# Convolution in 32-token blocks with two lag steps per matmul, in a kernel that runs attention and a long convolution side by side

## The chip, the cores and the metric

One core of a Trainium2 chip. The metric is the device time of one execution in microseconds; quoted times are medians. Ratios are computed as the mean time of one kernel's fast runs over the mean of the other's in the same rounds, so they are not quite the ratio of the medians beside them. One kernel's executions can differ by a per cent, so differences under 1% are not read as effects. A run counts as slow when its time is over 1.5% above the fastest run of the same kernel; the others are fast. The medians are over all runs of a kernel, slow ones included.

## The reference, cut to what matters

```python
x = A_x                                       # 1 x 2048 x 448
g = sigmoid((x * gate_w).sum(-1, keepdims=True))
a = attention(x, wq, wk, wv, wo)              # 16 heads of 28, one key/value head
K = einsum("dn,dnl,dn->dl", C, exp(dt*A*l), dt*B).real   # 448 channels x 2048 taps, 256 modes
y = causal_convolution(u, K) + u * Dskip      # every channel has its own taps
return g * a + (1 - g) * y
```

The device kernel reads A_x for both inputs. It computes the convolution as matmuls, channel by channel: shifted copies of the taps (`T`) are the moving operand, the tokens (`U`) the stationary one, also called the weights. The moving operand of one matmul is called a stream below. PSUM is the memory that takes the results of matmuls (`psS`, `psX` and `psB` in the profiles).

## The kernel before: the parts that matter

Every operation is handed to a small static scheduler, together with an expected duration in ns. The scheduler fixes the order of instructions on each engine before the kernel runs. A wrong duration gives no wrong result, but a poor order.

```python
def conv(self, c):                      # 16 channels, bank 5 of PSUM
    for k in range(4):
        gi = 4 * c + k; s = gi % self.NTR
        self.tload(gi)                  # 128 x 8 KB into one of four T buffers
        for m in range(1, 16, 2):
            def mm(e, ...):
                for j in range(4):      # four channels, one per 32-column tile
                    r = e.matmul(ps.v(32 * j, 33 - m, po + 128 * k, [[1, 128]]),
                                 self.U.v(0, P, (m - 1) * D + 4 * gi + j, [[D, 33 - m]]),            # weights
                                 self.T.v(0, P, s * 4096 + (960 - 64 * m) * 4 + j, [[4, 128]]),      # moving: step 4 elements = 8 bytes
                                 start=(m == 1), stop=(m == 15), tile_position=(0, 32 * j), ...)
            pg.op("pe", mm, 112, ...)   # scheduled as 112 ns per four matmuls
    # VectorE multiplies by (1 - g) into cst, ytr flips and sums on TensorE, VectorE adds to O
```

TensorE also runs the scores (L967 in the profile of before), probability times value (L985), the making of the taps (L792) and the projections (L676, L877). ScalarE runs the exponentials (L977). VectorE builds the tables from which the taps are made (L759, L762, L767, L776, L778). All of it is interleaved in one schedule.

## Time and profile before

| | before |
|---|---|
| time | 539.37 us (537.78 to 539.81) |
| busy: TensorE / VectorE / ScalarE | 484.8 / 483.9 / 487.5 us of a span of 537.2 |
| mean granted TensorE clock | 0.921 |
| convolution matmuls on TensorE | 142 us |
| scores + probability-value on TensorE | 144 + 78 us |
| TensorE idle | 39 us |

The granted clock is the share of TensorE's full clock that the chip let it run at; in all 14 clock records of this trace it is either full or half (1.00 or 0.50). The last three rows are read from the trace. Each matmul is given the time to the start of the next one, at most its own record, and what remains between the first matmul and the last is idle. This counts overlapped matmuls once, which the group rows of the page do not do. Three engines at 90% each is the main thing to see: by these shares none of the three stands out as the bound. The chain that ended last is shared by them too:

```profile
PE 47%; ACT 36%; DVE 12%; DMA 2%; issue 1%; POOL 1%; DVEq 0%; POOLq 0%
```

### The profile page before, as it was taken

What the parts mean: (1) busy time and instruction counts of PE and PEld (TensorE: products, weight loads), DVE (VectorE), ACT (ScalarE), POOL (GpSimd) and SP (SyncE); (2) the same over time, 40 slices, a digit from 0 to 9 for tenths busy, and PEclk for the clock granted to TensorE, in tenths of its full rate; (3) what the DMA queues carried; (4) which work ended last, traced back from release to release, by engine and by line L of the source; (5) the groups of instructions that cost most, each with busy time, mean ns of one, the idle gap of its engine ahead of it and who ended that gap; (6) DMA issues with size and microseconds to landing.
All of it is one profiled execution on the core that took longest, in us unless ns stands there. A gap on an engine that the chain in (4) does not pass through costs nothing.

```text
span 537.2 us, 18418 instructions
## 1 busy us (share of the span) xinstructions
PE 484.8 (90%) x8229; PEld 243.8 (45%) x8229; DVE 483.9 (90%) x1168; ACT 487.5 (91%) x428; POOL 4.9 (1%) x17
## 2 busy tenths in 40 slices
PE   6778888999999899999999999999999998998893
PEld 5411132553545444554545445554455543544452
DVE  4978899998999999999999999999999999999023
ACT  4599998998999999999999999999999999999960
POOL 3000000000000000000000000000000000000000
PEclk9855566997999999999999999999999999889997
DMA  8735445777798867779898896778877796697954
GB/s 232 145 79 137 138 139 207 245 285 299 249 327 297 303 230 237 253 265 345 304 337 320 262 332 238 242 260 319 309 296 267 285 393 220 176 388 254 350 188 137
DMA packets 42266, 138.16 MB, mean 257 GB/s; under 512 B 8168, under 2 KB 24476, under 8 KB 27852
## 3 DMA queue, kind: packets, MB, share of 16 engines
q1 hardware_dynamic: 40396, 135.71, 73.7%
q10 hardware_dynamic: 1792, 1.29, 0.8%
q8 instruction: 64, 1.05, 0.8%
q14 instruction: 14, 0.11, 0.1%
HBM read 133.01 MB, written 3.85 MB: 255 GB/s over the span
## 4 chain that ended last, share of the span: by engine, by line
PE 47%; ACT 36%; DVE 12%; DMA 2%; issue 1%; POOL 1%; DVEq 0%; POOLq 0%
ACT expT L977 35%; PE psS L967 13%; PE psS L853 12%; PE psB L985 8%; PE psX L792 6%; PE psX L676 2%; DMA T<-KP_scratch 2%; DVE tab L767 2%; DVE tmp L762 2%; DVE tab L759 2%; PE psS L504 1%; PE psX L877 1%; PE psX L831 1%; DVE O L883 1%; DVE tab L776 1%
## 5 line engine op out<-in xcount | busy, mean ns | idle before, releaser
L977 ACT ACTIVATE expT<-psS 128x1536 bf16<-128x1536 f32 (+1 forms) x410 | 470.8, 1254 | 19.0 <-PE psB L985 12.9
L967 PE MATMUL psS<-qT,kT 29*128 29x512 bf16 x1024 | 170.6, 412 | 29.6 <-ACT expT L977 27.2
L853 PE MATMUL psS<-T,U 128*26 128x128 bf16 (+7 forms) x3584 | 157.9, 303 | 0.6 <-DMA T<-KP_scratch 0.5
L853 PEld LDWEIGHTS psS<-T,U 128*26 128x26 bf16 (+7 forms) x3584 | 113.9, 152 | 35.3 <-issue 28.2
L985 PE MATMUL psB<-expT,vaug 128*32 128x512 bf16 x1024 | 108.8, 417 | 1.4 <-ACT gtok L643 1.3
L967 PEld LDWEIGHTS psS<-qT,kT 29*128 29x128 bf16 x1024 | 39.6, 92 | 124.4 <-ACT expT L977 92.8
L762 DVE TENSOR_TENSOR tmp<-tab,mbf 128x2048 bf16<-128x2048 bf16 (+4 forms) x140 | 78.0, 563 | 0.0
L759 DVE TENSOR_TENSOR tab<-tab,mbf 128x2048 bf16<-128x2048 bf16 (+4 forms) x140 | 77.9, 563 | 0.0
L767 DVE TENSOR_TENSOR tab<-tab,tmp 128x2048 bf16<-128x2048 bf16 (+4 forms) x140 | 77.8, 563 | 0.0
L792 PE MATMUL psX<-tab 128*32 128x96 bf16 x1792 | 54.8, 268 | 1.3 <-issue 1.2
L985 PEld LDWEIGHTS psB<-expT,vaug 128*32 128x32 bf16 x1024 | 26.6, 95 | 64.2 <-issue 60.8
L792 PEld LDWEIGHTS psX<-tab 128*32 128x32 bf16 x1792 | 41.2, 116 | 14.2 <-issue 9.0
L776 DVE TENSOR_TENSOR tab<-tab,mbf 128x2048 bf16<-128x2048 bf16 x28 | 34.0, 1216 | 0.0
L778 DVE TENSOR_TENSOR tab<-tab,mbf 128x2048 bf16<-128x2048 bf16 x28 | 34.0, 1213 | 0.0
L861 DVE TENSOR_TENSOR cst<-psS,omq 128x512 bf16<-128x512 f32 x28 | 19.0, 680 | 15.7 <-PE psS L853 15.5
L717 DVE TENSOR_TENSOR msq<-mst 128x256 f32<-128x256 f32 x63 | 26.2, 416 | 0.0
L676 PE MATMUL psX<-xT,Wq 112*128 112x512 bf16 x64 | 21.7, 436 | 0.4 <-DVE O L838 0.2
L727 DVE CAST mbf<-mst 128x256 bf16<-128x256 f32 x70 | 20.1, 288 | 0.1
L720 DVE TENSOR_TENSOR mst<-msq 128x128 f32<-128x128 f32 x70 | 19.7, 282 | 0.0
L723 DVE SCALAR_TENSOR_TENSOR mst<-mst 128x128 f32<-128x128 f32 x63 | 17.8, 283 | 0.0
L804 DVE TENSOR_REDUCE kstg<-psX 128x128 bf16<-128x256 f32 x28 | 11.7, 418 | 4.2 <-PE psX L792 4.1
L730 DVE TENSOR_SCALAR mbf<-mst 128x128 bf16<-128x128 f32 x70 | 15.3, 218 | 0.0
(112 smaller groups left out, 255.8 us busy)
## 6 DMA issues: line engine op xcount, KB each, us to landing
T<-KP_scratch SPq DMA_DIRECT2D x112, 1024.0 KB, 7.8
rdenB<-R_scratch SPq DMA_DIRECT2D x60, 64.0 KB, 3.8
U<-in_A_x_dram SPq DMA_DIRECT2D x3, 896.0 KB, 5.4
tab<-in_A_x_dram SPq DMA_DIRECT2D x4, 448.0 KB, 6.9
O<-Z_scratch SPq DMA_DIRECT2D x1, 1792.0 KB, 13.6
KP_scratch<-kstg SPq DMA_DIRECT2D x28, 64.0 KB
xT<-in_A_x_dram SPq DMA_DIRECT2D x1, 1792.0 KB, 9.2
U<-Z_scratch SPq DMA_DIRECT2D x1, 896.0 KB, 8.0
```

Of the source, the lines that this page charges most:

```text
L676: pg.op("pe", lambda e, T=T: e.matmul(px, self.Wq.v(0, DT, T * 512 + g * 128, [[1, 128]]), self.xT.v(0, DT, T * S + 512 * qc, [[1, 512]]), ...
L717: pg.op("dve", lambda e, k=k: e.tensor_tensor(msq.v(0, P, 0, [[1, 2 * BW]]) if k > 1 else msq.v(0, P, 0, [[BW, 2], [1, BW]]), src_both(k - ...
L759: pg.op("dve", lambda e, d=dst, a=src, ra=ra, w=w: e.tensor_tensor(d, a, mbf.v(0, P, ra, [[8, 16], [0, 2 * w], [1, 4]]), ALU.mult), el(n, ...
L762: pg.op("dve", lambda e, a=src, rb=rb, w=w: e.tensor_tensor(tmp.v(0, P, so, [[4 * w, 32], [1, 4 * w]]), a, mbf.v(0, P, rb, [[4, 32], [0, w ...
L767: pg.op("dve", lambda e, d=dst, t=t2: e.tensor_tensor(d, d, t, ALU.add), el(n, 1.92), rd=[("tmp", s), ("tab", s, lv + 1)], wr=[("tab", s, ...
L776: pg.op("dve", lambda e: e.tensor_tensor(ua, src, mbf.v(0, P, ra, [[8, 8], [0, 64], [1, 4]]), ALU.mult), el(2048, 1.92), rd=rk + mk, wr=[( ...
L778: pg.op("dve", lambda e: e.tensor_tensor(ub, src, mbf.v(0, P, rb, [[4, 16], [0, 32], [1, 4]]), ALU.mult), el(2048, 1.92), rd=rk + mk, wr=[ ...
L792: r = e.matmul(self.psX.v(32 * g, 32, 96 * jj, [[1, 96]]), tab.v(0, P, o + 768, [[4, 32]]), tab.v(0, P, o, [[256, 3], [4, 32]]), start=(co ...
L853: r = e.matmul(ps.v(32 * j, 33 - m, po + 128 * k, [[1, 128]]), self.U.v(0, P, (m - 1) * D + 4 * gi + j, [[D, 33 - m]]), self.T.v(0, P, s * ...
L967: r = e.matmul(self.psS.v(0, P, 1536 * s + 512 * k, [[1, 512]]), kT.v(32 * h, DH + 1, 128 * kt, [[1, 128]]), qT.v(32 * h, DH + 1, 512 * qs ...
L977: pg.op("act", lambda e: e.activation(expT.v(0, P, 512 * (i0 % 10), [[1, n]]), self.psS.v(0, P, 1536 * s, [[1, n]]), AF.Exp, scale=SQ), 75 ...
L985: r = e.matmul(self.psB.v(32 * h, 32, 0, [[1, 512]]), vaug.v(0, P, 32 * kt, [[1, 32]]), expT.v(0, P, 512 * ((4 * st + h) % 10), [[1, 512]] ...
```

## The change

The intent was to take time from TensorE and to move fewer bytes: pairs of 64-column matmuls in place of groups of four of 128 (the same number of matmuls over half the columns each), T loads half as large, weights that lie contiguously, results flipped and summed by one matmul with a flip matrix, fewer blocks of table powers. The diff, cut to its core:

```diff
-KPW = 2112
+KR = 68
+KPW = 256 * KR
...
-        sizes = [4] * 7
+        sizes = [2, 5, 7, 7, 7]
...
-        pg.dma([(self.T.v(0, P, s * 4096, [[1, 4096]]),
-                 dram(self.KP, 4 * gi * KPW, [[4, 64], [4096, 2], [1, 4096]]))],
-               (128, 8192), f"T{s}", rd=[("KP", c), "pad"], wr=[("T", s)], pr=1, ns=3300)
+        pg.dma([(self.T.v(0, P, s * self.TW, [[1, self.TW]]), dram(self.KP, gi * KPW, [[KR, 128], [1, self.TW]]))],
+               (128, 4096), f"T{s}", rd=[("KP", c)], wr=[("T", s)], pr=1, ns=1700)
...
-            for m in range(1, 16, 2):
-                def mm(e, k=k, m=m, s=s, gi=gi):
-                    for j in range(4):
-                        r = e.matmul(ps.v(32 * j, 33 - m, po + 128 * k, [[1, 128]]),
-                                     self.U.v(0, P, (m - 1) * D + 4 * gi + j, [[D, 33 - m]]),
-                                     self.T.v(0, P, s * 4096 + (960 - 64 * m) * 4 + j, [[4, 128]]),
-                                     start=(m == 1), stop=(m == 15), tile_position=(0, 32 * j), skip_group_check=True)
-                pg.op("pe", mm, 112, rd=[("T", s), "U"], ...
+            for k1 in range(2):
+                pr = 2 * q + k1
+                for mg in range(2):
+                    def mm(e, mg=mg, k1=k1, pr=pr, s=s):
+                        for m in range(4 * mg, 4 * mg + 4):
+                            M = max(34, 64 - 8 * m)
+                            for par in range(2):
+                                r = e.matmul(ps.v(64 * par, M, po + 64 * pr, [[1, 64]]),
+                                             self.U.v(0, P, uo + (32 * par + e0 + pr) * UC + 8 * m, [[1, M]]),
+                                             self.T.v(0, P, s * self.TW + 8 * m + 2 * k1 + par, [[4, 2], [KR, 32]]),
+                                             start=(m == 0), stop=(m == 7), tile_position=(0, 64 * par), skip_group_check=True)
+                    pg.op("pe", mm, 118, rd=[("T", s)] + ...
...
-    def ytr(self, c):                  # 16 small matmuls with an identity, per chunk
+    def jpass(self, c):                # two matmuls with a flip matrix
```

Cut away: the staging of the input in memory and its reversed reload as `U`, the output projection as two pairs of 224 columns, the skip connection, and some constants of the scheduler. The moving operand of the change is `[[4, 2], [KR, 32]]`: its inner dimension steps 68 elements, 136 bytes. Its tiling has two column tiles (64 wide) where before had four (32 wide). And 118 ns are scheduled for four pairs, about 30 ns a pair.

## The prediction

A "line" is an aligned stretch of 16 bytes in a partition of the moving operand. A "drain" is the time that a change of tiling adds, some 100 ns in the trace of before (315 ns from start to start against 216). What TensorE does in it is not shown.

> **What bounds the kernel now.** I read the page first (busy shares, slices, chain), then the groups, the waits of ScalarE and VectorE, the timeline of one warm stretch, and the start times of single instructions. The page gives three engines at nine tenths:
>
> ```profile
> PE 484.8 (90%) x8229; PEld 243.8 (45%) x8229; DVE 483.9 (90%) x1168; ACT 487.5 (91%) x428; POOL 4.9 (1%) x17
> ...
> PEclk9855566997999999999999999999999999889997
> ```
>
> The second row is the granted TensorE clock per slice; it is about half from slice 3 to slice 7, that is roughly from 22 to 94 us. The groups say which work this is:
>
> ```profile
> L977 ACT ACTIVATE expT<-psS 128x1536 bf16<-128x1536 f32 (+1 forms) x410 | 470.8, 1254 | 19.0 <-PE psB L985 12.9
> ...
> L853 PE MATMUL psS<-T,U 128*26 128x128 bf16 (+7 forms) x3584 | 157.9, 303 | 0.6 <-DMA T<-KP_scratch 0.5
> ...
> L792 PE MATMUL psX<-tab 128*32 128x96 bf16 x1792 | 54.8, 268 | 1.3 <-issue 1.2
> ```
>
> The exponentials (L977) fill ScalarE, and it idles only 19 us in front of them. But busy time hides something: back to back, a 1536-wide exponential starts 1330 ns after the last and a 1024-wide one 901 ns (10th percentile of the starts), while their records are longer because they overlap. Summed over the loop (33.6 to 519.5 us) the starts lie 32 us above that pitch: 12 us before 136 us, where the TensorE clock is half for long, 19 us from 136 to 470, and 1.3 us in the last 50 us. So ScalarE could save at most 32 us. Who holds it up:
>
> ```profile
> ACT expT L977 <- PE psB L985: 12.9, 27, 1.4
> ACT expT L977 <- PE psS L967: 4.4, 10, 0.7
> ```
>
> Both are TensorE being late. The timeline of TensorE shows why: pieces of the convolution (L853, 28 matmuls, about 0.9 us) lie between score matmuls (L967) and probability-value matmuls (L985).
>
> ```profile
> 228.62 0.39 PE L967 MATMUL psS<-qT,kT 29*128 29x512 bf16 x2
> 228.94 0.40 PE L985 MATMUL psB<-expT,vaug 128*32 128x512 bf16 x4
> 229.16 1.03 PE L853 MATMUL psS<-T,U 128*20 128x128 bf16 x28
> 230.12 0.39 PE L967 MATMUL psS<-qT,kT 29*128 29x512 bf16 x3
> ```
>
> VectorE is as full (162.1 of 164 us between 136 and 300 us), but its share of the work ends near 492 us; then it waits for the last two convolutions:
>
> ```profile
> DVE cst L861 <- PE psS L853: 15.5, 4, 12.2
> ```
>
> After the last exponential (519.5) there are 17.7 us of tail: normalisation, projection, the last convolution (its matmuls run to 527.9) and 7.4 us of stores issued at 529.8.
>
> [...] from a row-tiled L967 to a column-tiled L985 the starts are 315 ns apart, from L985 to L853 (same tiling) 216 ns, so a change costs some 100 ns. [...] L831 (64-column tiles, 64 wide) runs a pair every 33 ns, 16 ns each. [...] The trace hints that strides matter: four concurrent L853 matmuls of 128 columns (step 8 bytes) take 124 ns from start to start, four L792 of 96 columns (step 8 bytes) 91 ns, four L985 of 512 contiguous columns 216 ns. That is 0.95 ns a column against 0.42, nearly whatever the weight columns (121 ns at 18, 126 at 30), and the same at half clock (120 to 126 and 90 ns). So the array is not the limit there. [...] In the trace 512-byte packets took 33 ns on average, 64-byte ones 11 ns: 16 against 6 bytes per ns.
>
> **The change part by part.**
> Convolution on TensorE: before, 896 groups of four by 124 ns = 111 us. After, again 28 x 128 = 3584 matmuls, but in 1792 pairs of 64 columns. If a pair runs at L831's 33 ns: 59 us, 52 less. The tiling becomes that of two columns[...]: of 246 visits, some 140 have L985 or L792 beside them; 140 x 0.1 = 14 us more. Net about -38 us of TensorE, 8% of its time.
> Weights: U becomes contiguous in time; the loads with step 896 bytes (149 ns median) should drop towards the 110 ns of L831's contiguous 64 columns. They are hidden behind the matmuls anyway.
> Flip and sum: 28 x 8 pairs x 33 ns = 7.4 us become 28 x two matmuls of 256 columns, about 6 us. Output projection: 448 columns as two pairs of 224, the same streaming; its eviction is two instructions in place of one, VectorE about +1 us in all. The skip connection gets fewer multiplies on long rows and more short adds: even.
> Master tables: 5 blocks in place of 7, hence 2 x 52 fewer VectorE instructions. L717 (256 elements, 416 ns) against L720 (128, 282 ns) gives some 150 ns fixed, about half of it overlapping the next instruction: 104 x 70 ns = -7 us. The first block is of 2 chunks, so the first tables come some 4 us sooner.
> DMA: a T load goes from 1024 KB to 544 KB, 112 times: 115 MB become 61 MB. It adds 28 loads of U with 2048 rows of 61 to 64 elements, about 126 bytes. At 15 ns a packet these are 57,000 packets / 16 x 15 ns = 54 us of queue time over the run, against some 170 us saved by T (from 325 us of 8 KB packets). No transfer should hold TensorE.
> Start: a staged transpose to memory and reversed copies; perhaps +1.5 us on the way to the first exponential.
> On the path: less TensorE work shortens the delays of the exponentials. Of the 32 us I take back 14, not all: the half-clock stretch stays, and VectorE still has 477 us of work. The tail loses about 3 us, since the last convolution ends before the last exponential and three of the four stores can go early. 539.4 - 14 - 3 + 1 = 523.
>
> **The rivals.**
> A, as above: the pair runs at 33 ns. For it: L831 does so with 64-column tiles, and the change's own scheduler costs put 118 ns on four pairs. Time 515 to 531.
> B, the strided stream sets the pace. The new moving operand steps 136 bytes, one element per 16-byte line, where the old one had two. If the limit is lines, 256 lines in 124 ns before, a pair's 128 lines take 60 ns: 1792 x 60 = 108 us, nothing gained, plus 14 us of drains, and a fixed instruction order planned for half of it. Better constants in the planner, the shorter VectorE work and the earlier tail offset this: 531 to 552, about 540. For it: the 0.95 ns does not move with the clock, and loads of weights also get slower with their step. Against: the new tiling has half the streams, and the costs written into the change.
> C, each stream has its own limit of lines: 120 ns a pair, 215 us of convolution, TensorE becomes the only bound: above 600.
> D, VectorE takes over: with ScalarE freed, its 98% in the loop stops the gain. The chunk work ended at 492 us and loses 7, so this bites only below about 515.
>
> **Range and chances.** I give A 0.5, B 0.42, C 0.08. A is faster by over 2% (below 528.6) with 0.85; B with 0.12, and slower with 0.2; C is slower. Faster 0.425 + 0.05 = 0.48, slower 0.08 + 0.08 = 0.16, within 2% 0.36. The middle of the mixture is a little above A's: 527. Range 514 to 549; C lies outside it.
>
> **What would show it.** The deciding number is the start-to-start time of two consecutive pairs of the convolution in a warm stretch: 30 to 35 ns for A, 55 to 65 for B, about 120 for C. For A the idle before exponentials falls below 12 us, the excess of their starts over the back-to-back pitch from 32 to about 18, and the last matmul of the convolution comes before the last exponential. For B these stay near 19 and 32, and PE busy stays at 480 us or more. T loads of 544 KB should land in some 5 us (7.8 before). VectorE busy should be about 477. I am wrong if the U loads make TensorE wait, if the start to the first steady exponential (33.7 us) moves by over 3 us, or if the new drains cost more than 100 ns each.

## The result, and the profile after

The changed kernel takes **693.04 us** (689.59 to 697.21, four runs) against 538.58 (535.97 to 539.81) in the same rounds: ratio 1.288, 95% interval 1.278 to 1.298. The result is correct. The prediction said 527.

The page of the changed kernel: the busy row and the granted clock, then the groups of the exponentials, the convolution, the scores, and the VectorE instruction that takes the convolution's results.

```profile
PE 624.0 (91%) x8034; PEld 343.0 (50%) x8048; DVE 489.4 (71%) x1085; ACT 496.3 (72%) x428; POOL 7.8 (1%) x15
...
PEclk9755559999877999999788997899799999855555
...
PE 68%; DVE 15%; ACT 15%; DMA 1%; issue 1%; SPq 0%
...
L1023 ACT ACTIVATE expT<-psS 128x1536 bf16<-128x1536 f32 (+1 forms) x410 | 479.6, 1240 | 158.7 <-PE psS L1013 94.3
L891 PE MATMUL psS<-T,U 128*34 128x64 bf16 (+4 forms) x3584 | 248.8, 303 | 1.0 <-issue 0.8
L1013 PE MATMUL psS<-qT,kT 29*128 29x512 bf16 x1024 | 186.6, 454 | 38.6 <-ACT expT L1023 35.4
...
L900 DVE TENSOR_TENSOR cst<-psS,omq 128x512 bf16<-128x512 f32 x28 | 19.4, 692 | 111.6 <-PE psS L891 111.6
```

TensorE alone is near nine tenths now; the exponentials wait 159 us, nearly all of it for TensorE (19 before), VectorE 112 us for the convolution alone. The convolution row grew from 157.9 to 248.8 us though every matmul has half the columns, and the mean record is 303 ns in both. The timeline of a warm stretch shows the pace (start, duration, engine, line, count):

```profile
228.78 0.40 PE L1031 MATMUL psB<-expT,vaug 128*32 128x512 bf16 x4
229.11 1.15 PE L891 MATMUL psS<-T,U 128*64 128x64 bf16 x16
...
230.19 0.39 PE L1013 MATMUL psS<-qT,kT 29*128 29x512 bf16 x2
```

Sixteen matmuls are eight pairs, and the next matmul starts 1.08 us after the first pair: with some 0.1 us of that a change of tiling, a pair every 120 ns or so. Taken pair by pair from the starts in the trace, the median is 122 ns, with 121 to 124 at every weight width from 34 to 64, and the same at full and at half clock. (Matmuls of the same pair start together.) This is the number the prediction called deciding: 30 to 35 for A, 55 to 65 for B, about 120 for C.

Where the 150 us between the two profiled spans are, by the counting of the table above (all matmuls that it does not name fit in the third row):

| TensorE, us | before | after | |
|---|---|---|---|
| convolution | 142.4 | 237.5 | +95 |
| scores + probability-value | 222.1 | 261.1 | +39 |
| all other matmuls (taps, projections, flip) | | | about +5 |
| idle | 39.2 | 49.1 | +10 |
| before the first matmul and after the last | 13.2 | 14.6 | +1 |

Most of the +39 is the clock. From start to start, a 512-column matmul of the query projection takes 216 ns at the full clock and 427 at the half, and the mean clock fell from 0.921 to 0.828: 646 of the 2048 score and value matmuls ran at half clock, against 254 before. With the times per matmul of the kernel before at each clock, that alone gives +29. The other 10 are the change of tiling: from the last value matmuls to the first of the convolution 329 ns pass in place of 227 at the full clock (546 in place of 400 at the half), 86 times. So two things are to be explained: the 122 ns, and the clock.

### The profile page after: what moved, and what is told of

Read it like the earlier page. It is cut to its first block, busy times and chain, and to the rows that moved or that the text cites. A ratio compares the mean times of both kernels' runs of the same rounds, so it can differ in the third digit from the quotient of the medians.

```text
span 687.7 us, 18049 instructions
## 1 busy us (share of the span) xinstructions
PE 624.0 (91%) x8034; PEld 343.0 (50%) x8048; DVE 489.4 (71%) x1085; ACT 496.3 (72%) x428; POOL 7.8 (1%) x15
## 4 chain that ended last, share of the span: by engine, by line
PE 68%; DVE 15%; ACT 15%; DMA 1%; issue 1%; SPq 0%
PE psS L891 34%; PE psS L1013 15%; ACT expT L1023 14%; PE psB L1031 9%; PE psX L828 4%; PE psX L709 2%; DVE tab L803 2%; DVE tab L795 1%; DVE tmp L798 1%; PE psX L918 1%; DMA tab<-in_A_x_dram 1%; DVE msq L752 1%; PE psS L531 1%; PE psX L865 1%; DVE cst L900 1%; PE psS L918 1%
## 5 line engine op out<-in xcount | busy, mean ns | idle before, releaser
L891 PE MATMUL psS<-T,U 128*34 128x64 bf16 (+4 forms) x3584 | 248.8, 303 | 1.0 <-issue 0.8
L1013 PE MATMUL psS<-qT,kT 29*128 29x512 bf16 x1024 | 186.6, 454 | 38.6 <-ACT expT L1023 35.4
L891 PEld LDWEIGHTS psS<-T,U 128*34 128x34 bf16 (+4 forms) x3584 | 197.8, 122 | 45.5 <-issue 43.2
L803 DVE TENSOR_TENSOR tab<-tab,tmp 128x128 bf16<-128x128 bf16 (+4 forms) x140 | 79.2, 566 | 0.7
L798 DVE TENSOR_TENSOR tmp<-tab,mbf 128x128 bf16<-128x128 bf16 (+4 forms) x140 | 78.9, 564 | 0.0
L795 DVE TENSOR_TENSOR tab<-tab,mbf 128x128 bf16<-128x128 bf16 (+4 forms) x140 | 78.3, 565 | 0.5
L752 DVE TENSOR_TENSOR msq<-mst 128x448 f32<-128x448 f32 (+2 forms) x45 | 23.6, 524 | 0.0
L870 DVE TENSOR_TENSOR O<-O,psX 128x256 bf16<-128x256 bf16 x28 | 11.6, 416 | 9.2 <-PE psX L865 9.1
L763 DVE CAST mbf<-mst 128x448 bf16<-128x448 f32 (+2 forms) x50 | 17.1, 342 | 0.1
L756 DVE TENSOR_TENSOR mst<-msq 128x224 f32<-128x224 f32 (+2 forms) x50 | 16.9, 338 | 0.0
```

Source lines behind the costliest of these rows:

```text
L752: pg.op("dve", lambda e, k=k: e.tensor_tensor(msq.v(0, P, 0, [[1, 2 * BW]]) if k > 1 else msq.v(0, P, 0, [[BW, 2], [1, BW]]), src_both(k - ...
L795: pg.op("dve", lambda e, d=dst, a=src, ra=ra, w=w: e.tensor_tensor(d, a, mbf.v(0, P, ra, [[8, 16], [0, 2 * w], [1, 4]]), ALU.mult), el(n, ...
L798: pg.op("dve", lambda e, a=src, rb=rb, w=w, so=so: e.tensor_tensor(tmp.v(0, P, so, [[4 * w, 32], [1, 4 * w]]), a, mbf.v(0, P, rb, [[4, 32] ...
L803: pg.op("dve", lambda e, d=dst, t=t2: e.tensor_tensor(d, d, t, ALU.add), el(n, 1.92), rd=[("tmp", lv % 2), ("tab", s, lv + 1)], wr=[("tab" ...
L891: r = e.matmul(ps.v(64 * par, M, po + 64 * pr, [[1, 64]]), self.U.v(0, P, uo + (32 * par + e0 + pr) * UC + 8 * m, [[1, M]]), self.T.v(0, P ...
L1013: r = e.matmul(self.psS.v(0, P, 1536 * s + 512 * k, [[1, 512]]), kT.v(32 * h, DH + 1, 128 * kt, [[1, 128]]), qT.v(32 * h, DH + 1, 512 * qs ...
```

## The experiments

Theory: a moving operand costs a fixed time for every new 16-byte line, in every stream by itself (the prediction's rival C). Rivals: the limit is shared by all streams (B), the smaller tiles or the weights set the pace, or the two-dimensional address. And for the rest of the loss: the half clock, the fixed order, or another engine.

### The read step: a_contig, a_steps, b_wide, b_step2

**a_contig** changes only how the moving operand of the changed kernel is read (wrong result):

```diff
-self.T.v(0, P, s * self.TW + 8 * m + 2 * k1 + par, [[4, 2], [KR, 32]])
+self.T.v(0, P, s * self.TW + 8 * m + 2 * k1 + par, [[1, 64]])
```

> The changed kernel, but the moving operand of the convolution is read contiguously (64 neighbouring elements in place of step 136 bytes); the result is wrong on purpose, everything else stays. Theory S (step): each stream of a moving operand gets one 16-byte line per 1.9 ns, so the strided pair takes 64 x 1.9 = 120 ns; contiguous, a pair takes 30 to 35 ns and the time falls from 693 to 518 to 535 us. Rival T (tiling): two column tiles of 64 with weights of 34 to 64 columns cost 120 ns a pair whatever is read; the pair stays at 120 and the time at 690. Rival R (rest): the pair goes to 33 ns, but the drains, the loads of U or the planned order hold the time above 600 us.

Measured: 568.09 us (564.05 to 574.72), before 539.22 in the same rounds, ratio 1.058 (1.048 to 1.068). A pair comes every 29 to 30 ns at the full clock (52 after the pair with the widest weights, 64 columns) and every 53 to 55 at the half; the convolution takes 87 us of TensorE in place of 237. So the step explains about 125 of the 154 us. Tiles, weights and the places of the results are the same as in the change, so they do not set the 122 ns; VectorE's instructions come in the same order too. (One of the four runs was slow.) But the time did not fall to 518-535; some 29 us above before are left for the second question.

**a_steps** gives each of the eight channel pairs of a T buffer another step (wrong on purpose, one look), each on its own source line; L892 has the change's own operand, but runs the four matmuls of one tile and then the four of the other, in place of alternating.

```diff
+if pr == 0:   r = e.matmul(*a, tv([[1, 64]]), **kw)     # L901: 2 bytes
+elif pr == 1: ... tv([[2, 64]])                         # L903: 4 bytes
+elif pr == 2: ... tv([[4, 64]])                         # L905: 8 bytes
+elif pr == 3: ... tv([[8, 64]])                         # L907: 16 bytes
+elif pr == 4: ... tv([[32, 64]])                        # L909: 64 bytes
+elif pr == 5: ... tv([[KR, 32], [4, 2]])                # L911: lag pair inside
+elif pr == 6: ... tv([[4, 2], [KR, 32]])                # L913: as in the change
+else: tile after tile                                   # L892: as in the change
```

> The changed kernel with another way of reading in each of the eight channel pairs of a chunk, each from its own source line (wrong result on purpose): step 2, 4, 8, 16 and 64 bytes; the right elements with the two lags innermost; the right elements as in the change; and as in the change but four matmuls of one tile before the four of the other. Theory S with a limit per stream: start to start of a pair 33, 33, 60, 120, 120 ns; lags innermost 80 to 100 (half of its element pairs lie in two lines); as is 120; tile after tile about 700 ns for eight matmuls in place of 480. If the limit were shared by the two streams, tile after tile would stay at 480 and step 8 bytes would take 30. Rival T: all 120. Time 590 to 640 us under S.

The groups of TensorE by line (busy us, mean ns of one record):

```profile
L892 PE MATMUL psS<-T,U 128*64 128x64 bf16 (+1 forms) x448 | 34.1, 301 | 0.0
L913 PE MATMUL psS<-T,U 128*64 128x64 bf16 (+1 forms) x448 | 34.0, 303 | 0.3 <-issue 0.3
L909 PE MATMUL psS<-T,U 128*64 128x64 bf16 (+1 forms) x448 | 32.1, 287 | 0.0
L907 PE MATMUL psS<-T,U 128*64 128x64 bf16 (+1 forms) x448 | 32.0, 294 | 0.5 <-DVE tab L803 0.5
L911 PE MATMUL psS<-T,U 128*64 128x64 bf16 (+1 forms) x448 | 26.6, 269 | 0.0
L905 PE MATMUL psS<-T,U 128*64 128x64 bf16 (+1 forms) x448 | 19.9, 237 | 0.5 <-DVE tab L795 0.3 <-DVE acc L998 0.3
L901 PE MATMUL psS<-T,U 128*64 128x64 bf16 (+1 forms) x448 | 15.5, 213 | 0.0
L903 PE MATMUL psS<-T,U 128*64 128x64 bf16 (+1 forms) x448 | 15.2, 209 | 0.0
```

The same 448 matmuls stand on every line, so the rows compare directly: equal at 2 and 4 bytes, more at 8, and from 16 bytes on a plateau. Start to start, a pair takes 29 ns at 2 bytes and 33 at 4 at the full clock (53 at the half), and at both clocks 59 at 8 bytes, 115 at 16, 110 at 64, 123 as in the change, and 90 with the lag pair inside. It stops growing at 16 bytes, the step where every column has a line of its own (115 ns, and 110 at 64 bytes). The two-dimensional address is not the point: 16 bytes in one dimension cost nearly the same. Tile after tile was a miss: eight matmuls take about 480 ns as in the alternating order, not the 700 I had written. Nor was it the test that it was meant to be. In the trace the two matmuls that start together have weights of the same width (64 and 64, then 56 and 56), and in the first half of a channel pair's matmuls each width occurs once per tile. So the two tiles ran side by side, though the kernel's text has the four of one tile first; where the order changed is not shown. By what I had written, the 480 spoke for a limit shared by the streams and the 59 ns at 8 bytes against it.

**b_wide** puts the same question to the kernel before, with four streams: a step of 64 bytes in place of 8 (wrong on purpose, one look). **b_step2** goes the other way and is correct: the taps of two channels are interleaved in memory in place of four, so the step is 4 bytes.

```diff
 # b_wide
-self.T.v(0, P, s * 4096 + (960 - 64 * m) * 4 + j, [[4, 128]])
+self.T.v(0, P, s * 4096 + j, [[32, 128]])
 # b_step2 (the stores of the taps and the T load follow the same layout, as two DMAs each in place of one)
-self.T.v(0, P, s * 4096 + (960 - 64 * m) * 4 + j, [[4, 128]])
+self.T.v(0, P, s * 4096 + j // 2 * 2048 + (960 - 64 * m) * 2 + j % 2, [[2, 128]])
```

> The kernel before, with one thing of the change put in alone: its moving operand steps 64 bytes in place of 8 (wrong result on purpose), the tiling, order, loads and weights stay. Theory S per stream: a group of four goes from 124 to 128 x 1.9 = 243 ns, the convolution from 111 to 218 us, the time from 539 to 630 to 690 us, and the granted clock falls as in the changed kernel. If lines are shared by the four streams, a group takes twice that, 490 ns, and the time passes 800. Rival T and R: no change, 124 ns and 539 us.

> The kernel before, with the taps of two channels interleaved in place of four, so that the moving operand steps 4 bytes in place of 8; right result. Theory S: four elements a line, a group of four takes max(0.42, 1.9 / 4) x 128 = 61 ns in place of 124, the convolution 55 us in place of 111, no drain added; fewer late score matmuls, time 512 to 528 us, and it beats both kernels. Under T nothing changes: 124 ns, 539 us. If VectorE is the bound behind TensorE, the group falls to 61 ns but the time stays above 530.

The convolution group and the granted clock, b_wide first:

```profile
PEclk9755669989999999999999999999999999999998
...
L853 PE MATMUL psS<-T,U 128*32 128x128 bf16 (+7 forms) x3584 | 258.8, 416 | 1.5 <-issue 1.3
```

and b_step2:

```profile
PEclk9765566995999699999898999999887997888597
...
L853 PE MATMUL psS<-T,U 128*32 128x128 bf16 (+7 forms) x3584 | 121.7, 251 | 2.5 <-DVE cst L861 0.5
```

b_wide: a group of four every 236 ns (124 before), 621.32 us, just under the 630 to 690 expected. b_step2: in the median 62 ns at the full clock with the narrowest weights, 87 with the widest, and 107 at the half clock (whether the loads of the weights, with step 896 bytes, play a part in this at the full clock, no run tests); 545.19 us, ratio 1.011 (1.005 to 1.017). That is the miss that matters: a read of the taps that took 30 us off the convolution did not make the kernel faster. (It also changed the order of instructions; see below.) And the clock went the other way than I had written: it rose in b_wide (0.941) and fell in b_step2 (0.858).

### The law inside the change, with a right result: a_pair72

If two columns share a line, the changed kernel's pair should take half the time. The lag pair goes inside, and a row has 72 lags, so that rows begin on 16 bytes; the VectorE instruction that takes the results puts the columns back in order.

```diff
-KR = 68
+KR = 72
-self.T.v(0, P, s * self.TW + 8 * m + 2 * k1 + par, [[4, 2], [KR, 32]])
+self.T.v(0, P, s * self.TW + 8 * m + 2 * k1 + par, [[KR, 32], [4, 2]])
-e.tensor_tensor(cst [[64, 8], [1, 64]], ps [[64, 8], [1, 64]], omq [[0, 8], [1, 64]], ALU.mult)
+e.tensor_tensor(cst [[64, 8], [32, 2], [1, 32]], ps [[64, 8], [1, 2], [2, 32]], omq [[0, 8], [32, 2], [1, 32]], ALU.mult)
```

> The changed kernel with the same right result, but the pair of lag steps is the inner dimension of the moving operand and a row holds 72 lags, so that consecutive columns lie 8 bytes apart (two to a 16-byte line) in place of 136. Theory 'a column costs 1.9 ns per stream when it lies in its own 16-byte line, half as much when two share one': a pair of matmuls every 58 to 64 ns at the full clock, 124 in the change; convolution 115 to 135 us in place of 237; time 585 to 615 us, less than the arithmetic 693 - 110 would give only if the half clock does not come with it. Rival 'what counts is that the address steps in two dimensions, or the jump between the rows': the lags-innermost order of 68 read 90 ns already, so it stays near 90 to 124 and the time at 640 or more.

Measured: 578.48 us (575.95 to 580.59), correct, ratio to before 1.070 (1.061 to 1.078). A pair every 60 ns, in the median, at both clocks and all weight widths. Convolution 126 us. So 115 us of the loss come back with little but another order of reading, somewhat more than expected (585 to 615 us). L911 of a_steps read in this order too, but with rows of 68 lags: every second row then begins in the middle of a 16-byte line, its pairs lie in two lines, and a pair of matmuls took 90 ns. The step inside a pair is 8 bytes in both; what differs between 90 and 60 ns is how many lines are touched, 48 or 32. The group:

```profile
L891 PE MATMUL psS<-T,U 128*34 128x64 bf16 (+4 forms) x3584 | 136.4, 237 | 3.1 <-issue 2.0
```

### One stream in the full array: b_full

a_steps left open whether the limit belongs to a stream or to all streams together. b_full reads the query projection of the kernel before (512 columns, whole array, one stream) in other steps, each input block on its own line (wrong).

```diff
+if T == 1: return e.matmul(px, w, xv([[4, 512]]), **kw)              # L681: 8 bytes
+if T == 2: return e.matmul(px, w, xv([[0, 4], [16, 128]]), **kw)     # L683: 32 bytes
+if T == 3: return e.matmul(px, w, xv([[0, 2], [2, 256]]), **kw)      # L685: 4 bytes
+return e.matmul(px, w, xv([[1, 512]]), **kw)                         # L686: contiguous
```

> The kernel before with the query projection's 512-column moving operand (full tiling, one stream) read in other steps, wrong result on purpose; each of the four input blocks has its own source line: contiguous, 4 bytes with every column pair twice, 8 bytes, and 32 bytes. If a stream is limited to one new 16-byte line per 1.9 ns whatever the tiling: about 480 ns at 8 bytes and 970 at 32. If the limit is for TensorE's whole front end (0.47 ns a line as with four streams): 216 to 240 ns at both. If two matmuls can be read at a time (0.95 ns a line): 240 and 480.

The durations, min/median/max:

```profile
L681 PE MATMUL psX<-xT,Wq x16: 610/612/636, 17.1 to 442.0; 112*128 112x512 bf16 x16
...
L683 PE MATMUL psX<-xT,Wq x16: 1075/1097/1097, 17.5 to 442.4; 112*128 112x512 bf16 x16
...
L685 PE MATMUL psX<-xT,Wq x16: 407/409/608, 18.4 to 443.4; 112*128 112x512 bf16 x16
...
L686 PE MATMUL psX<-xT,Wq x16: 389/390/607, 16.8 to 441.4; 112*128 112x512 bf16 x16
```

From start to start: 225 ns contiguous, 432 at 8 bytes, 917 at 32. Near the 480 and 970 of the limit per stream, and far from the 216-240 of one shared limit and from the 240 and 480 of two. (552 us for the kernel, because of these longer matmuls.) All readings together, with the lines that one matmul touches in a partition:

| matmuls | streams | step | lines each | ns from start to start | ns per line |
|---|---|---|---|---|---|
| before, convolution | 4 | 8 B | 64 | 124 | 1.9 |
| before, taps (L792) | 4 | 8 B | 48 | 91 | 1.9 |
| b_wide | 4 | 64 B | 128 | 236 | 1.8 |
| after | 2 | 136 B | 64 | 122 | 1.9 |
| a_steps, L907 | 2 | 16 B | 64 | 115 | 1.8 |
| a_steps, L911 | 2 | lag pair inside, rows of 68 | 48 | 90 | 1.9 |
| a_steps, L905 | 2 | 8 B | 32 | 59 | 1.8 |
| a_pair72 | 2 | 8 B | 32 | 60 | 1.9 |
| b_full, L683 | 1 | 32 B | 512 | 917 | 1.8 |
| b_full, L681 | 1 | 8 B | 256 | 432 | 1.7 |

One, two or four streams: 1.7 to 1.9 ns per new line in each stream. (At 4 bytes, with 16 lines for 64 columns, it hardly shows: 33 ns a pair, against 29 contiguous.) Before, a stream had 64 lines for 128 columns; the change made it 64 lines for 64 columns with half as many streams at a time. So the convolution takes twice as long: 896 x 124 = 111 us became 1792 x 122 = 219.

### Why a cheap read gains nothing, first try: a_twice

a_contig had a convolution 56 us shorter than before and was 29 us slower. My theory was the clock: a TensorE with less to do gets the half clock. a_twice gives it back some work: a_contig with every convolution matmul issued twice (wrong).

```diff
-for m in range(4 * mg, 4 * mg + 4):
+for m, tw in [(m, tw) for m in range(4 * mg, 4 * mg + 4) for tw in range(2)]:
```

> The changed kernel with a contiguous moving operand (wrong result on purpose) and every convolution matmul issued twice, so that TensorE has the work of about 60 ns per pair in place of 30. It is to tell why the contiguous form still took 568 us, 29 more than the kernel before. Theory 'a TensorE with less to do is granted the half clock, and the score and value matmuls at half clock make the exponentials late': with about 55 us more of work the clock rises from 0.815 to 0.87 or more, the score and value matmuls take 20 us or more less in sum, and the time stays within 12 us of 568 in spite of the work. Rival 'the order of the instructions or VectorE holds it, the clock is only a sign': the clock may rise but the time rises by 25 us or more, to 590 to 620.

Measured: 626.58 us (621.59 to 633.32), 58 more than a_contig. The clock rose only to 0.841, scores and probability-value fell by 4 us. In this form the theory fails. The test is also disturbed: 30 us of idle time inside the doubled convolution show "issue" as their cause, so TensorE was not kept evenly busy. It showed where to look: not at the amount of work, but at gaps. I went through the clock records of 18 traces in windows of 3.41 us (from 60 us on, without the last 25 us; in the traces of before and after each of these records but the last lasts a whole multiple of 3.41 us), each with its busy share and the clock of the window after it:

| busy share of a window | at full clock: windows, clock falls next | at half clock: windows, clock rises next |
|---|---|---|
| under 0.65 | 102, 90 | 21, 5 |
| 0.65 to 0.80 | 270, 77 | 57, 1 |
| 0.80 to 1.00 | 816, 2 | 188, 45 |
| 1.00 | 865, 0 | 257, 127 |

So in these traces a window at the full clock with 1.2 us or more of idle time (35% of 3.41) was mostly followed by the half clock (90 of 102), whether that time lay in one gap or in several (68 of the 90 had no gap that long); with 0.7 to 1.2 us it was in 77 of 270. The way back often took more than one busy window: 127 of 257 fully busy ones were followed by a rise. The share of the records does not tell all: in the changed kernel the clock stayed at half for 82 us, from 598 to 680, with TensorE busy for 78.92 of them. What else decides is not shown.

b_wide, the kernel before and b_step2 read with steps of 64, 8 and 4 bytes. The step from b_wide to before is clean: all 1137 compute instructions of VectorE come in the same order. That to b_step2 is not: its T loads and stores of taps are two DMAs each, the scheduler counts them, and from the 191st instruction of VectorE on it chose another order. The series:

| | b_wide | before | b_step2 |
|---|---|---|---|
| convolution, us of TensorE | 241 | 142 | 113 |
| TensorE idle, us | 34 | 39 | 64 |
| mean clock | 0.941 | 0.921 | 0.858 |
| scores + probability-value, us | 218 | 222 | 238 |
| time, us | 621 | 539 | 545 |

The 30 us taken from the convolution in b_step2 went into 25 us of idle time and 16 us of slower matmuls; how much of that comes from the other order is not tested. Of the idle time in b_step2, 39 us are score matmuls waiting for ScalarE to free their banks (27 before).

### The order: a_pair72p and b_step2p

The schedule counts on a duration per step. In a_pair72 a step of four pairs was counted 118 ns and takes 240; in b_step2 a group was counted 112 and takes 60 to 100. Both get one number corrected (both correct):

```diff
 # a_pair72p
-pg.op("pe", mm, 118, ...
+pg.op("pe", mm, 240, ...
 # b_step2p
-pg.op("pe", mm, 112, ...
+pg.op("pe", mm, 60, ...
```

> The run a_pair72 (right result, 578 us, a pair every 60 ns) with one number of the static schedule set right: a step of four pairs counted 118 ns, is now counted 240 as measured. The change's own schedule counted 118 ns for four pairs, about 30 ns a pair, so its order was made for a convolution twice as fast as in a_pair72 and four times as fast as in the change itself. Theory 'the order was made for the wrong duration: exponentials wait behind convolution stretches that were thought short': ScalarE's wait for score and value matmuls falls from 55 us to under 30, and the time from 578 to 550-565. Rival 'the half clock alone makes the rest': unchanged within 1% of 578.

> The interleaved kernel b_step2 (right result, 545 us) with the schedule told 60 ns for a convolution group in place of 112. If its order for the old duration kept the gain away: 525 to 535. If VectorE and ScalarE bind, or the half clock eats it: 538 to 550, with TensorE waiting for expT as before.

a_pair72p: 577.2 us (574.9 to 577.8), unchanged. Yet the wait of the exponentials did what the theory said. The waits of ScalarE (total us, times, longest), a_pair72 first:

```profile
ACT expT L1023 <- PE psS L1013: 30.2, 49, 1.9
ACT expT L1023 <- PE psB L1031: 25.3, 39, 1.6
```

and a_pair72p:

```profile
ACT expT L1023 <- PE psB L1031: 15.4, 25, 1.7
ACT expT L1023 <- PE psS L1013: 10.1, 20, 1.3
```

The wait went from 55 to 25 us, and the last exponential ended at 530 in place of 563 us. But the convolution was pushed back: 512 of its matmuls came after the last exponential (none in a_pair72), and the span ended at 575. A loss in the loop was turned into a tail of the same size. b_step2p: 551.39 us (549.17 to 558.29), ratio of the fast runs 1.019; no better than b_step2. Its profile fell in a slow run, so I read no more from it.

### The other engines: b_blocks6, b_blocks6s2, b_less, b_less2, b_act, b_al, b_al2

If ScalarE or VectorE takes away what TensorE gains, lightening them should show it. First with right results: fewer and larger blocks of table powers, one part of the change, which needs room, so that one scratch buffer and one of the four T buffers go. b_blocks6s2 has the interleaved taps of b_step2p as well.

```diff
-        self.NTR = 4
+        self.NTR = 3
-        self.tmp = sb("tmp", 2 * 2048, BF)
+        self.tmp = sb("tmp", 2048, BF)
-        sizes = [4] * 7
+        sizes = [4] + [6] * 4
```

> The kernel before, right result, with 5 blocks of powers for the tables (4, 6, 6, 6, 6 chunks) in place of 7 of 4: 104 VectorE instructions fewer at an estimated 120 to 150 ns of fixed cost each, 12 to 15 us less VectorE; to make room one scratch buffer of the tables and one of four T buffers go. TensorE's work is unchanged. Theory 'VectorE is as much the bound as TensorE and ScalarE': 524 to 534 us, 1 to 3% faster. Rival 'TensorE's order of instructions or ScalarE's 487 us of exponentials hold it': within 1% of 539. The three T buffers could cost something if TensorE waits for T.

> The kernel before with both reliefs, right result: the taps of two channels interleaved (moving operand step 4 bytes, a group of four in 60 to 100 ns in place of 124, with the planner told 60) and 5 blocks of powers in place of 7. If VectorE is what took the 30 us of TensorE away in the interleaved kernel (545 us), both together give 515 to 530 us, clearly below either alone. If the half clock took it, the time is at or above that of the five blocks alone, with a mean clock of 0.88 or less.

The 120 to 150 ns of fixed cost were my estimate from the trace of before: 416 ns for 256 elements (L717) and 282 for 128 (L720) leave 148 for none. Both missed: 582.55 us (ratio 1.078) and 568.38 (1.050). VectorE did get through early: the table of the last chunk was done at 476 us in place of 486. But the last exponential ended no sooner (522 us), and 492 convolution matmuls were left for after it. TensorE now waits for T (total us, times, longest):

```profile
PE psS L853 <- DMA T<-KP_scratch: 20.7, 11, 5.0
```

So this pair says nothing on VectorE; the wait for T points to the missing fourth T buffer, but the halved scratch was not tested by itself. The next runs take work away without touching buffers (wrong). b_less leaves out two VectorE products per chunk, 67 us in all; b_act makes each exponential an eighth narrower after the first ten tiles, about 55 us of ScalarE; b_al does both. b_less2 and b_al2 are b_less and b_al with the interleaved taps of b_step2p.

```diff
 # b_less, b_al: tables, level 4 without its cross products
+            if lv == 4:
+                continue
 # b_act, b_al
-            n = 512 * len(ts)
+            n = (512 if i0 < 10 else 448) * len(ts)
```

> The kernel before with 56 VectorE instructions of about 1.2 us left out (two of the table's products at the last level; wrong result on purpose), 67 us less VectorE. TensorE's and ScalarE's work is unchanged. If VectorE is a bound of its own: 520 to 530 us, where ScalarE's 487 us of work and its start at 22 us then hold it. If TensorE holds the kernel before by itself: 536 to 542.

> The same lighter VectorE (wrong result on purpose) with the interleaved taps and the 60 ns of b_step2p. It tells what the 30 us of TensorE that the smaller read step frees are worth once VectorE does not bind. If VectorE took them away: 510 to 525 us and below b_less. If the half clock takes them away: at or above b_less, with a mean clock under 0.88 and over 12 us more on score and value matmuls than in the kernel before.

> The kernel before with every exponential (after the first ten tiles) over 448 columns per tile in place of 512 (wrong result on purpose): 55 us less ScalarE, TensorE and VectorE unchanged. If ScalarE alone is the bound of the kernel before: 500 to 520 us. If VectorE and TensorE, both at 484 us of work, bind right behind it: 525 to 536.

> Both ScalarE (55 us) and VectorE (67 us) lightened, convolution as before (wrong result on purpose): only TensorE is left as the bound, 485 us of work with some 30 us of start and end: 510 to 525 us, with the clock at 0.92 or more. It is the base for b_al2.

> b_al with the interleaved taps (moving step 4 bytes, 60 ns in the schedule): TensorE has 30 to 40 us less work while nothing else binds. Theory 'a cheaper read pays where TensorE alone binds': 475 to 500 us, at least 15 below b_al. Rival 'the half clock takes it back wherever TensorE has idle time': within 10 us of b_al, with the mean clock below 0.88.

| lightened | run | time, us | ratio to before (95%) | last exponential ends | convolution matmuls after it |
|---|---|---|---|---|---|
| nothing | before | 539 | 1 | 519 | 64 |
| TensorE | b_step2p | 551.39 | 1.019 (1.014 to 1.024) | | |
| VectorE | b_less | 538.04 | 0.999 (0.991 to 1.007) | 516 | 64 |
| ScalarE | b_act | 552.86 | 1.024 (1.017 to 1.031) | 479 | 720 |
| VectorE + TensorE | b_less2 | 547.42 | 1.014 (1.010 to 1.017) | 534 | 0 |
| VectorE + ScalarE | b_al | 548.91 | 1.017 (1.012 to 1.023) | 475 | 768 |
| all three | b_al2 | 532.66, in the one fast run 523.26 | none, three of four runs slow | 473 | 448 |

No single engine is the bound: 67 us less VectorE gained nothing, because the exponentials still ended at 516; 55 us less ScalarE ended the exponentials 40 us sooner and left 720 convolution matmuls for the end, where they run alone and wait for T, and the clock falls, as the slices of b_act show (ScalarE, and below it the clock, in 40 slices of the span):

```profile
ACT  4598888899999999998999999999999999600000
...
PEclk9765566799999999998999999999999999998666
```

The half clock is not what this tail costs: a group at 8 bytes a step keeps its pace of 120 to 126 ns at half clock. In b_al TensorE waits 22 us for T after 475 us, at a DMA share of 0.76 to 1.01. So another limit, the T loads, comes up there; no run makes them smaller in a lightened kernel.

b_less2 met what had been written for the half clock: slower than b_less, mean clock 0.859, and 22 us more on score and value matmuls than in the kernel before.

Only b_al2 is clearly below the kernel before: its four runs (523.26 to 533.44) lie below the four of b_al (546.15 to 549.40), by 16 us in the medians and by 26 in its one fast run. So a cheaper read of the moving operand does pay where ScalarE and VectorE leave room: 43 us less convolution, with the new order that goes with it, bring 16 to 26. The 475 to 500 us that I had expected were missed, and so was the 510 to 525 of b_al, which was meant to leave TensorE alone as the bound: it too ended with a tail. No version with a right result was faster than the kernel before.

## Why the prediction was wrong, point by point

**The step that failed** is the first of the sum: "If a pair runs at L831's 33 ns: 59 us, 52 less." Measured: 122 ns a pair; 1792 of them are 219 us, where the sum had 59 and the kernel before 111 (by the table of TensorE, 237 in place of 142). The 33 ns were real but were read from the wrong instruction: L831's moving operand is an identity with step 4 bytes, sixteen columns to a run, and a_steps shows that 4 bytes cost next to nothing (33 ns, 29 contiguous) while 8 cost 59. I had the right suspicion and noted 0.95 ns a column for both strided groups of before. But everything strided in before ran in four streams at 8 bytes, so that profile could not tell a shared limit (B) from one per stream (C). I gave C, which named the outcome in numbers (120 ns, above 600), a chance of 0.08 with no evidence against it, and counted the 118 ns in the diff as evidence for A. They are the author's estimate, and the trace shows the step of four pairs to take about 490.

**The step of before** was slow already: its 8 bytes put two bf16 columns in a line, and a column took 0.95 ns, against 0.42 for contiguous ones. This was in my own prediction, and I gave the case "one column per line, and each stream by itself" only 0.08.

**14 us back from ScalarE**: not in the change, where it lost 140 (the wait before exponentials went from 19 to 159 us) as TensorE had 139 us more to do, 95 of them convolution; and not with the cheap reads either (a_contig, b_step2). There the clock was lower (0.815 and 0.858, 0.921 before), TensorE had more idle time, and scores come later: the series b_wide, before, b_step2 shows idle time (34, 39, 64 us) and the time of scores and probability-value (218, 222, 238 us) growing as the convolution shrinks, though b_step2 has another order too. How much of a_contig's +29 us is clock (40 us more for scores and probability-value, some 10 of them the change of tiling) and how much idle time (34 us more) is not parted by any run.

**Rival D**, VectorE takes over: not so. b_less has 67 us less of it and is no faster. What binds is the three engines together; that the fixed order serves attention first and leaves what is late to the tail is my reading of the tails, which no run tests by itself.

**VectorE busy about 477**: 489.4. The larger blocks did save the 7 us: with overlaps counted once, the five lines of the table powers (L717 to L730) took 78.3 us before and 71.1 after. But what I had called even was not: the split evictions of the projection (+2.8), the set-up (+2.6), the skip connection (+1.7), the convolution's results (+2.4) and the tables themselves (+3.4) took more than that back.

**The details**: a T load of 544 KB lands in 4.0 us ("some 5"). A new change of tiling costs 102 ns at the full clock and 146 at the half (329 and 546 ns from value matmuls to the convolution, 227 and 400 before), 10 us in all where the sum had 14. The U loads make TensorE wait nowhere in the list of waits. The first exponential comes 7 us later than before (29.5 us in place of 22.5), but the sixth at 35.9 us in both. The DMA sum was off: its own figures give 152 us saved by T, not 170; measured were 133, and the U rows took 92 us and not 54 (21 to 32 ns a packet in place of 15). None of this mattered beside the pace of a pair.

## What to carry to other kernels

Before a layout is changed so that a matmul reads its moving operand with a step, count the 16-byte lines that a stream touches, not the columns: here each cost 1.7 to 1.9 ns per stream, and fewer, narrower streams made it worse (two of 64 columns took 122 ns, four of 128 took 124). A measured duration of another matmul is evidence only if its operands have the same step and the same tiling: L831 ran a pair in 33 ns at 4 bytes, the change took 122 at 136. Where three engines were at 90% under a fixed order, as here, time saved on one of them came back as idle time and a slower clock (b_step2: 25 us more idle, a clock of 0.858 against 0.921) or as a tail (b_act: 720 convolution matmuls after the last exponential); lighten all that bind, and set the durations of the schedule again from a trace.
